# Layer norm of the first segment moved behind the projections: only its mean goes in ahead of the transposes

## The chip, the cores and the metric

The kernel runs on one core of one Trainium2 chip. The metric is the device time of one execution in microseconds (us), as the median of several runs. TensorE (PE) multiplies matrices into PSUM, which has eight banks; VectorE (DVE), ScalarE (ACT) and GpSimd (POOL) do the rest; SyncE (SP) issues the DMAs. Each engine works through its own instructions in order, and waits on semaphores for the others.

## The reference: what is computed

One transformer block on x of 2048 tokens by 1024 features, in two halves. The first half is h = x + A(layernorm(x)), the second h + B(layernorm(h)).

```
# A: 4 segments of 512 tokens, 32 heads of width 32
q, k, v = x @ wq, x @ wk, x @ wv
per segment s:
    p     = softmax(q_s k_s^T * 32**-0.5 + causal mask)
    a_dot = p @ v_s
    a_mem = phi(q_s) M / (phi(q_s) z + 1e-6)      # M, z: sums over the earlier segments
    o_s   = sigmoid(beta) * a_mem + (1 - sigmoid(beta)) * a_dot
    M, z  = M + phi(k_s)^T v_s, z + sum phi(k_s)
A = concat(o_s) @ wo
# B: gelu(x @ w_in), half of it layer-normed and mixed over the tokens by w_sp, times the other half, @ w_out
layernorm(x) = (x - mean(x)) / sqrt(var(x) + 1e-5)  # over the 1024 features of a token
```

The layer norm has no weights of its own. So its factor 1/std belongs to a token: it can be applied to x, or as well to the row of v, and to the column of the transposed q and k, that the token gives.

## The kernel before, in words

The program is written as one list of instructions in source order; a recorder works out the semaphore waits from the tiles that each instruction reads and writes, and puts every instruction at the end of its engine's queue. All instructions have the line of that recorder's call (L209) in the profile, so they are told apart by engine, operation and tiles. A transfer is issued by SP in source order, and waits there for the readers of the tile that it overwrites.

**The opening** works on segment 0, the first 512 tokens, as four chunks of 128 tokens (`XCH[0]` to `XCH[3]`, tile `xch`). SP issues the four loads of x, then the weights: the first half of w_v in two pieces of 256 columns (`WV[0]`), 256 columns each of w_k and w_q, beta, the second half of w_v (`WV[1]`). PE runs 12 idle matmuls on a zeroed tile (`warm(12)`, tile `etmp`), then more of them (`warm(3)`, `warm(2)`) between the first steps. For each chunk:

- `stats_of(tc)`: two BATCH_NORM_STATS2 and one BATCH_NORM_AGGREGATE on DVE (tiles `stats`, `mv`: mean and variance), then two small operations on POOL (tile `rs`: the variance plus epsilon, and that to the power of -0.5).
- `ln_apply`: one DVE operation, x minus the mean times 1/std, to tile `lno`.
- `pe_T`: eight PE transposes of `lno` into PSUM and their copy to the transposed tile `xnT` (by ACT; for the first chunk one half by ACT, the other by DVE).
- `v_quarter`: two groups of eight matmuls (128x256) give half 0 of v for the chunk (columns 0 to 511 of 1024), and ACT copies each group to tile `v`.

For chunk 3 the two `v_quarter` come after `proj_qk(0, 1)` and `proj_qk(0, 0)`, eight matmuls (128x512) each, which give k and q of the first quad transposed; ACT copies them to tile `qk`. `gates()` works out sigmoid(beta) on ACT and DVE. `phi_exp` (ACT) and `phi_max` (DVE, three operations, tiles `pqk` and `etmp`) give phi(k), and SP issues a DMA transpose of it (tile `pk`).

**The quads.** A quad is 4 heads; 8 quads per segment, numbered n = 0 to 31. Quad n is this fixed order of PE work: `logits(n, 0)`; filler f1; `pv(n-1)` (probabilities times v, 40 matmuls); `logits(n, 1)`; `state(n-1)` (phi(k) times v); filler f2; `logits(n, 2)`; filler f3; filler f4. In segment 0 f1 is k and f2 is q of quad n+1, f3 is a 512-column v product. Each `logits` writes PSUM banks 0 to 3, and ACT takes the exponential of all four banks in one instruction (tile `e`), so a `logits` waits for the exponential before it. POOL sets the upper triangle to zero. The fillers take turns with banks 6 and 7. On DVE, quad n has in this order: the norm of quad n-1 after `pv(n-1)` (tiles `rd`, `otok`), two operations after `state` (`msum`, `mzb`), then background work on the next segment's layer norm (`bg_pop`: `stats` of one chunk in each of quads 0 to 3, later its `lno`), then `phi_max(n+1)`. In quad 0 alone, DVE also builds a mask of 13 operations (`mask_g`, tile `maskg`) after the third `logits` and before `phi_max(1)`.

From the second segment on the same quads run with other fillers. Then the second half of the block (tiles `win`, `z`, `z1T`, `wspT`, `w_out`, `yT`), which is PE work end to end, takes the rest of the time.

Of the kernel before, what the change touches and what calls it, by code (L numbers as in the profile page):

```python
# [5 lines left out]
BF16 = mybir.dt.bfloat16  # L6
F32 = mybir.dt.float32
I32 = mybir.dt.int32
ACTF = mybir.ActivationFunctionType
ALU = mybir.AluOpType  # L10

T = 2048
D = 1024
H = 32
NSEG = 4
L = 512
# [3 lines left out]
NQ = 8  # L20
SCALE = 32 ** (-0.5)
LN_EPS = 1e-5
# [235 lines left out]
def bass_sequential_preLN__memory_aug_infini_attn__mixer_gmlp__prompt_kernel(  # L258
# [17 lines left out]
    pe, act, dve, pool, sp = R.pe, R.act, R.dve, R.pool, R.sp  # L276
# [39 lines left out]
    RS = [cb("rs%d" % i, [128, 2], F32) for i in range(4)]  # L316
    RD = cb("rd", [128, 4, 4], F32)
    RDM = cb("rdm", [128, 4, 4], F32)


    HNT = [tens("hnT0", [128, 8, L], BF16, 14 * K), tens("hnT1", [128, 8, L], BF16, 22 * K),
# [8 lines left out]
    HCH = [b1("hch%d" % i, [128, D], BF16) for i in range(3)]  # L330
    LNO = [b1("lno%d" % i, [128, D], BF16) for i in range(3)]
    OT = b1("oT", [128, NQ, L], BF16)
    b2 = Bump(134 * K, ARENA)
    ZSTG = [tens("zstg%d" % i, [128, 448], F32, (134 + 2 * i) * K) for i in range(4)]
    XCH = [b2("xch%d" % i, [128, D], BF16) for i in range(4)]
# [28 lines left out]
    def bank(b):  # L364
        return PS[:, b, :]
# [6 lines left out]
    def next_bank():  # L372
        b = rot["banks"][rot["n"] % len(rot["banks"])]
        rot["n"] += 1
        return b

    def mm8(dst, lhs, rhs, n=8):
        for i in range(n):
            pe.matmul(dst, lhs(i), rhs(i), start=(i == 0), stop=(i == n - 1))
# [5 lines left out]
    def wcols(ap, lo, hi):  # L385
        return ap[:, lo:hi].rearrange("(c p) n -> p c n", p=128)

    for tc in range(4):
        x_load(tc)
    sp.dma_start(WV[0][:, :, 0:256], wcols(A_wv, 0, 256))  # L390
    sp.dma_start(WV[0][:, :, 256:512], wcols(A_wv, 256, 512))
    sp.dma_start(WK[:, :, 0:256], wcols(A_wk, 0, 256))
    sp.dma_start(WQ[:, :, 0:256], wcols(A_wq, 0, 256))
    sp.dma_start(BETAB[:], A_beta.partition_broadcast(128))
# [6 lines left out]
    pool.iota(IOT[:], [[1, 128]], base=0, channel_multiplier=-1)  # L401
    pool.memset(V[:, :, :, 32:34], 1.0)
    pool.memset(BLK[:], 1.0)
    pool.affine_select(out=BLK[:], in_=BLK[:], pattern=[[-32, 4]], compare_op=ALU.is_ge, fill=0.0, base=0,
                       channel_multiplier=1)
    pool.affine_select(out=BLK[:], in_=BLK[:], pattern=[[32, 4]], compare_op=ALU.is_ge, fill=0.0, base=31,
# [20 lines left out]
    def ln_stats(src):  # L427
        k = lnc[0] % 4
        lnc[0] += 1
        for i in range(2):  # L430
            dve.bn_stats(STATS[k][:, i, :], src[:, i * 512:(i + 1) * 512])
        dve.bn_aggr(MV[k][:], STATS[k][:])
        return k

    def ln_rstd(k):
        pool.tensor_single_scalar(RS[k][:, 0:1], MV[k][:, 1:2], float(LN_EPS), ALU.add)
        pool.tensor_tensor(RS[k][:, 1:2], RS[k][:, 0:1], MHALF[:], ALU.pow)
# [3 lines left out]
    def ln_apply(src, k):  # L441
        o = LNO[lno[0] % 3]
        lno[0] += 1
        dve.tensor_scalar(o[:], src[:], MV[k][:, 0:1], RS[k][:, 1:2], ALU.subtract, ALU.mult)
        return o
# [4 lines left out]
    def pe_T(dst, tcl, src, engines=(act,)):  # L450
        w = 8 // len(engines)
        for k, eng in enumerate(engines):
            bb = bank(next_bank()).bitcast(BF16)[:, 0:w * 128]
            for i in range(w):
                o = (k * w + i) * 128
                pe.transpose(bb[:, i * 128:(i + 1) * 128], src[:, o:o + 128], IDENT[:])
            d = dst[:, k * w:(k + 1) * w, tcl * 128:(tcl + 1) * 128]
            v = bb.rearrange("p (c n) -> p c n", c=w)
            if eng is act:
                act.activation(d, v, ACTF.Copy)  # L460
            else:
                dve.tensor_copy(d, v)


    def proj_v(s, tcl, half):
        proj_v_cols(s, tcl, half * 512, 512)

    def proj_v_cols(s, tcl, lo, w):
        b = next_bank()
        xt = XNT[s % 2]  # L470
        mm8(PS[:, b, 0:w], lambda i: xt[:, i, tcl * 128:(tcl + 1) * 128], lambda i: WV[lo // 512][:, i, lo % 512:lo % 512 + w])
        act.activation(V[:, tcl, lo // 32:(lo + w) // 32, 0:32],
                       PS[:, b, 0:w].rearrange("p (h d) -> p h d", d=32), ACTF.Copy)

    def proj_qk(n, which):
        s, c = divmod(n, NQ)
        b = next_bank()
        xt = XNT[s % 2]
        w = WK if which else WQ
        mm8(bank(b), lambda i: w[:, i, c * 128:(c + 1) * 128], lambda i: xt[:, i, :])  # L480
        act.activation(QK[n % 2][:, which, :], bank(b), ACTF.Copy)

    def phi_views(n):
        s = n // NQ
# [17 lines left out]
    def logits(n, rnd):  # L502
        qk = QK[n % 2]
        parts = {0: ((0, 0, 512),), 1: ((1, 0, 384), (3, 384, 128)), 2: ((2, 0, 256),)}[rnd]
        wid = (512, 512, 256)[rnd]
        e = E[n % 2][rnd]
        for j, o, w in parts:
            for i in range(4):
                pe.matmul(PS[:, i, o:o + w], qk[32 * i:32 * (i + 1), 1, j * 128:(j + 1) * 128],
                          qk[32 * i:32 * (i + 1), 0, j * 128:512], start=True, stop=True,  # L510
                          tile_position=(32 * i, 0))
        if rnd == 2 and n >= NQ:
            mem(n)
        act.activation(e[:, :, 0:wid], PS[:, 0:4, 0:wid], ACTF.Exp, scale=float(SCALE))
        for j, o, w in parts:
            d = e[:, :, o:o + 128]
            pool.affine_select(out=d, in_=d, pattern=[[0, 4], [1, 128]], compare_op=ALU.is_ge, fill=0.0,
                               base=0, channel_multiplier=-1)
        if rnd == 2 and n >= NQ:
            mem_norm(n)  # L520
# [84 lines left out]
            lnq[1].append(it + (ln_stats(it[0]),))  # L605


    ks = {}

    def stats_of(tc):  # L610
        ks[tc] = ln_stats(XCH[tc])
        ln_rstd(ks[tc])

    def warm(k):
        for _ in range(k):
            pe.matmul(bank(7), IDENT[:], ETMP[:, 0, :], start=True, stop=True)

    def v_quarter(tcl, q):
        proj_v_cols(0, tcl, 256 * q, 256)

    warm(12)
    stats_of(0)
    stats_of(1)
    ln0 = ln_apply(XCH[0], ks[0])
    pe_T(XNT[0], 0, ln0, (act, dve))
    warm(3)
    ln1 = ln_apply(XCH[1], ks[1])
    stats_of(2)
    pe_T(XNT[0], 1, ln1)
    warm(2)  # L630
    stats_of(3)
    v_quarter(0, 0)
    v_quarter(0, 1)
    ln2 = ln_apply(XCH[2], ks[2])
    ln3 = ln_apply(XCH[3], ks[3])
    pe_T(XNT[0], 2, ln2)
    v_quarter(1, 0)
    v_quarter(1, 1)
    pe_T(XNT[0], 3, ln3)
    v_quarter(2, 0)  # L640
    v_quarter(2, 1)
    for tc in range(4, 8):
        x_load(tc)
    sp.dma_start(WK[:, :, 256:D], wcols(A_wk, 256, D))
    sp.dma_start(WQ[:, :, 256:D], wcols(A_wq, 256, D))
    gates()
    proj_qk(0, 1)
    proj_qk(0, 0)
    v_quarter(3, 0)
    v_quarter(3, 1)  # L650
    phi_exp(0)
    phi_max(0)
    rot["banks"] = [6, 7]
# [39 lines left out]
    for n in range(LAST + 1):  # L693
        s, c = divmod(n, NQ)
        f1, f2, f3, f4 = [], [], [], []
        if n < LAST:
            f1, f2 = [("qk", n + 1, 1)], [("qk", n + 1, 0)]
        if s == 0:
            f3 = [("v", 0, c, 1)] if c < 4 else [("v", 1, c - 4, 0)]
        elif s < NSEG - 1:  # L700
            if c < 2:
                f3, f4 = [("v", s, 2 * c, 1)], [("v", s, 2 * c + 1, 1)]
            elif c < 6:
                f3, f4 = [("wo", s - 1, c - 2, 0)], [("wo", s - 1, c - 2, 1)]
            else:
                f3, f4 = [("v", s + 1, 2 * (c - 6), 0)], [("v", s + 1, 2 * (c - 6) + 1, 0)]
        elif c < 2:
            f3, f4 = [("v", s, 2 * c, 1)], [("v", s, 2 * c + 1, 1)]
        elif c < 6:
            f3, f4 = [("wo", s - 1, c - 2, 0)], [("wo", s - 1, c - 2, 1)]  # L710
        elif c == 6:
            f3, f4 = [("z2", 0, 4, 0)], [("z2", 0, 5, 1)]
        else:
            f1, f2 = [("z2", 0, 6, 2)], [("z2", 0, 7, 3)]
            f3, f4 = [("z2", 0, 0)], [("z2", 0, 1)]

        def fill(lst):
            for u in lst:
                {"v": proj_v, "wo": wo, "qk": proj_qk, "z2": z2_group}[u[0]](*u[1:])

        if s < NSEG - 1 and c < 4:
            ln_tasks(XCH[c], XNT[(s + 1) % 2], c)
        if s < NSEG - 2 and c >= 4:
            x_load(4 * (s + 2) + c - 4)
        if s > 0 and c == 1:
            xr_load(4 * (s - 1))

        logits(n, 0)
        fill(f1)
        if n > 0:  # L730
            pv(n - 1)
        logits(n, 1)
        if n > 0:
            state(n - 1)
        bg_pop()
        fill(f2)
        logits(n, 2)
        if n == 0:
            mask_g()
        if n < LAST:  # L740
            phi_exp(n + 1)
        while n == LAST and staged:
            z2_gelu(*staged.pop(0))
        fill(f3)
        if n < LAST:
            phi_max(n + 1)
        bg_pop()
        fill(f4)
        bg_pop()
        if n == 1:  # L750
            sp.dma_start(WO[:], wcols(A_wo, 0, D))
        if n in (24, 26):
            win_load((n - 24) // 2)
# [101 lines left out]
```

## Time and profile before

| | |
|---|---|
| median of 6 runs | 805.44 us (805.33 to 805.56) |
| the profiled execution's own time | 805.33 us |
| its span in the trace | 803.6 us |
| PE busy | 791.3 us, 98% |
| DVE, ACT, POOL busy | 368.0, 302.9, 121.0 us |
| opening, up to the first `logits` on PE | 0 to 21.89 us |
| quad 0 | 21.89 to 29.16 us |
| quads 1 and 2 | 29.16 to 36.77, 36.77 to 44.37 us |

Busy shares are means over stages. The span is that of the trace; what the measured time has beyond it lies around the span. Times below are microseconds from the span's start. In the timeline a line is a start, a duration, an engine, an operation, its output and inputs and a count; in brackets stands how long the engine had been idle and what released it. A matmul's shown duration holds its way through the array: matmuls of 512 columns start some 0.21 us apart while each is shown with 0.38.

### The profile page before, as it was taken

What the parts mean: (1) busy time and instruction counts of PE and PEld (TensorE: products, weight loads), DVE (VectorE), ACT (ScalarE), POOL (GpSimd) and SP (SyncE); (2) the same over time, 40 slices, a digit from 0 to 9 for tenths busy, and PEclk for the clock granted to TensorE, in tenths of its full rate; (3) what the DMA queues carried; (4) which work ended last, traced back from release to release, by engine and by line L of the source; (5) the groups of instructions that cost most, each with busy time, mean ns of one, the idle gap of its engine ahead of it and who ended that gap; (6) DMA issues with size and microseconds to landing.
All of it is one profiled execution on the core that took longest, in us unless ns stands there. A gap on an engine that the chain in (4) does not pass through costs nothing.

```text
span 803.6 us, 12469 instructions
## 1 busy us (share of the span) xinstructions
PE 791.3 (98%) x5337; PEld 384.1 (48%) x5407; DVE 368.0 (46%) x756; ACT 302.9 (38%) x360; POOL 121.0 (15%) x234
## 2 busy tenths in 40 slices
PE   8999999999999999999999999999999999999998
PEld 5445544555554445455544444444444444444444
DVE  4653688669854675844563000054234323423332
ACT  3888876887787666133333333100000000000000
POOL 2342433234322331100131000000000000000000
PEclk9999999999999999999999999999999999999999
DMA  9672544454415323621116000550270044011002
GB/s 296 157 172 60 92 80 119 80 99 81 99 41 126 113 54 69 188 60 53 53 53 131 1 1 0 194 114 1 79 138 1 26 105 86 1 59 53 1 7 86
DMA packets 125992, 64.79 MB, mean 81 GB/s; under 512 B 94832, under 2 KB 114928, under 8 KB 125936
## 3 DMA queue, kind: packets, MB, share of 16 engines
q1 hardware_dynamic: 125936, 63.99, 33.9%
q8 instruction: 42, 0.69, 0.3%
q14 instruction: 14, 0.11, 0.1%
HBM read 32.51 MB, written 8.39 MB: 51 GB/s over the span
## 4 chain that ended last, share of the span: by engine, by line
PE 92%; DVE 4%; ACT 2%; issue 1%; DMA 0%
PE ps L209 92%; ACT e L209 2%; DVE stats L209 1%; DVE ta L209 0%; DVE otok L209 0%; DVE hch L209 0%; DMA xch<-in_A_x_dram 0%; DVE lno L209 0%; DVE mv L209 0%; DVE rd L209 0%; DVE pqk L209 0%; DVE mzb L209 0%; DVE rdm L209 0%; DVE msum L209 0%; DVE etmp L209 0%
## 5 line engine op out<-in xcount | busy, mean ns | idle before, releaser
L209 PE MATMUL ps<-wspT,z 128*128 128x512 bf16 x878 | 193.1, 379 | 0.9
L209 ACT ACTIVATE e<-ps 128x2048 bf16<-128x2048 f32 (+1 forms) x96 | 152.8, 1591 | 46.1 <-PE ps L209 45.8
L209 PEld LDWEIGHTS ps<-wspT,z 128*128 128x128 bf16 x896 | 87.7, 98 | 105.7
L209 DVE TENSOR_TENSOR tmpg<-ps,brow 128x512 f32<-128x512 f32 x56 | 38.7, 691 | 197.0 <-DMA brow<-in_B_b_sp_dram 104.6
L209 POOL TENSOR_SCALAR_AFFINE_SELECT e<-e 128x512 bf16<-128x512 bf16 x128 | 81.3, 647 | 195.2 <-ACT e L209 195.2
L209 PE MATMUL ps<-win,hnT 128*128 128x448 bf16 x512 | 98.3, 352 | 0.0
L209 PE MATMUL ps<-w_out,yT 128*128 128x512 bf16 (+1 forms) x453 | 96.9, 372 | 0.5
L209 PE MATMUL ps<-hnT,win 128*128 128x512 bf16 x439 | 96.2, 379 | 0.5
L209 PEld LDWEIGHTS ps<-win,hnT 128*128 128x128 bf16 x512 | 49.8, 98 | 46.5 <-issue 0.4
L209 PEld LDWEIGHTS ps<-w_out,yT 128*128 128x128 bf16 x462 | 45.2, 98 | 51.7
L209 PEld LDWEIGHTS ps<-hnT,win 128*128 128x128 bf16 x448 | 43.8, 98 | 52.8
L209 PE MATMUL ps<-xnT,wk 128*128 128x512 bf16 x255 | 60.6, 380 | 0.1
L209 PE MATMUL ps<-wv,xnT 128*128 128x512 bf16 (+1 forms) x288 | 59.0, 356 | 0.0
L209 ACT ACTIVATE z<-ps 128x448 bf16<-128x448 f32 x60 | 32.5, 543 | 69.4 <-PE ps L209 69.4
L209 PE MATMUL ps<-wo,oT 128*128 128x512 bf16 x254 | 57.6, 379 | 0.1
L209 ACT ACTIVATE z1T<-ps 128x512 bf16<-128x512 f32 x56 | 33.4, 597 | 63.3 <-PE ps L209 63.3
L209 PE MATMUL ps<-xnT,wq 128*128 128x512 bf16 x225 | 53.8, 379 | 2.4 <-DVE rd L209 0.6
L209 DVE TENSOR_TENSOR fin<-fin,ps 128x512 bf16<-128x512 bf16 (+1 forms) x33 | 22.1, 672 | 71.5 <-DMA fin<-out_dram 38.7
L209 DVE BATCH_NORM_STATS2 zst<-z 128x6 f32<-128x448 bf16 x64 | 38.9, 620 | 30.1 <-ACT z L209 30.1
L209 ACT ACTIVATE qk<-ps 128x512 bf16<-128x512 f32 x64 | 38.4, 599 | 6.6 <-PE ps L209 6.6
L209 PEld LDWEIGHTS ps<-v,e 128*128 128x128 bf16 x1280 | 36.7, 96 | 7.4
L209 DVE TENSOR_TENSOR yT<-tmpg,z1T 128x512 bf16<-128x512 f32 x56 | 38.8, 692 | 1.9
(67 smaller groups left out, 568.0 us busy)
## 6 DMA issues: line engine op xcount, KB each, us to landing
xch<-in_A_x_dram SPq DMA_DIRECT2D x16, 256.0 KB, 3.6
xr<-in_A_x_dram SPq DMA_DIRECT2D x16, 256.0 KB, 3.7
out_dram<-hch SPq DMA_DIRECT2D x16, 256.0 KB, 2.4
fin<-out_dram SPq DMA_DIRECT2D x16, 256.0 KB, 2.8
out_dram<-fin SPq DMA_DIRECT2D x31, 128.0 KB, 1.7
win<-in_B_w_in_dram SPq DMA_DIRECT2D x4, 896.0 KB, 5.0
w_out<-in_B_w_out_dram SPq DMA_DIRECT2D x1, 3584.0 KB, 12.7
win<-in_B_w_in_dram SPq DMA_DIRECT2D x3, 1024.0 KB, 5.2
```

The costliest lines, as they stand in the source:

```text
L209: ins = getattr(e, op.name)(*op.args, **op.kw)
```

## The change

Segment 0 alone is affected. Its x is centered (the mean is subtracted) before the transposes, and no longer divided by the standard deviation there. 1/std of each token (`RS0`, a column per chunk) is applied later: to v as the scale of the ACT copy out of PSUM (`v_out`), and to k and q, whose tokens lie along the columns, by a DVE multiplication with a tile `RB` that has the 512 values of 1/std in every row (`qk_out`; in the eight quads of segment 0 it takes the place of the ACT copy). `RB` is made by PE: a matrix of ones times two diagonal matrices (`DIAG`, the high and the low part of 1/std in bf16), copied out by ACT.

The means of chunks 1 to 3 come from ACT (`act_mean`: a copy with an accumulator output), and so does the variance of chunk 3 (`act_var`: a square with an accumulator output). Chunks 0 to 2 keep the DVE statistics, chunks 1 and 2 for the variance alone, at a later place. The 128x256 v products become 128x512; those of chunks 0 and 1 go through their eight row blocks side by side, in parts of five and three, with the transposes of chunk 2 between. Half 0 of v for chunk 3 moves into quad 0 as filler f1, and k of quad 1 to the front of `logits(0, 0)`. The first half of w_v is loaded in four pieces of 256 rows. `warm(3)` is gone. For each chunk's transposed halves, the first is copied by ACT and the second by DVE (chunk 0: both by DVE).

```diff
-    sp.dma_start(WV[0][:, :, 0:256], wcols(A_wv, 0, 256))
-    sp.dma_start(WV[0][:, :, 256:512], wcols(A_wv, 256, 512))
+    for i in range(0, 8, 2):
+        sp.dma_start(WV[0][:, i:i + 2, :],
+                     A_wv[i * 128:(i + 2) * 128, 0:512].rearrange("(c p) n -> p c n", p=128))
...
+    pool.memset(ONES[:], 1.0)
...
+    def v_out(s, tcl, half, b):
+        act.activation(V[:, tcl, 16 * half:16 * half + 16, 0:32], bank(b).rearrange("p (h d) -> p h d", d=32),
+                       ACTF.Copy, scale=RS0[tcl][:] if s == 0 else 1.0)
...
-        act.activation(QK[n % 2][:, which, :], bank(b), ACTF.Copy)
+        qk_out(n, which, b)
+
+    def qk_out(n, which, b):
+        if n < NQ:
+            dve.tensor_tensor(QK[n % 2][:, which, :], bank(b), RB[:], ALU.mult)
+        else:
+            act.activation(QK[n % 2][:, which, :], bank(b), ACTF.Copy)
...
+    def center(tc, mean, op=ALU.add):
+        o = LNO[tc % 3]
+        dve.tensor_single_scalar(o[:], XCH[tc][:], mean, op)
+        return o
+    def act_mean(tc):
+        act.activation(JUNK[:], XCH[tc][:], ACTF.Copy, scale=-1.0 / D, accum_out=MEAN[tc][:])
+    def act_var(tc):
+        act.activation(JUNK[:], XCH[tc][:], ACTF.Square, bias=MEAN[tc][:], accum_out=RS[tc][:, 1:2])
+        pool.tensor_scalar(RS[tc][:, 0:1], RS[tc][:, 1:2], 1.0 / D, float(LN_EPS), ALU.mult, ALU.add)
+    def var0(k):
+        pool.tensor_single_scalar(RS[k][:, 0:1], MV[k][:, 1:2], float(LN_EPS), ALU.add)
+    def rstd0(tc):
+        pool.tensor_tensor(RS0[tc][:], RS[tc][:, 0:1], MHALF[:], ALU.pow)
+        pool.tensor_single_scalar(DIAG[0][:, tc, :], IDENT[:], RS0[tc][:], ALU.mult)
+    def diag_lo(tc):
+        dve.scalar_tensor_tensor(DIAG[1][:, tc, :], IDENT[:], RS0[tc][:], DIAG[0][:, tc, :], ALU.mult, ALU.subtract)
...
     warm(12)
-    stats_of(0)
-    stats_of(1)
-    ln0 = ln_apply(XCH[0], ks[0])
-    pe_T(XNT[0], 0, ln0, (act, dve))
-    warm(3)
-    ln1 = ln_apply(XCH[1], ks[1])
-    stats_of(2)
-    pe_T(XNT[0], 1, ln1)
-    warm(2)
-    stats_of(3)
-    v_quarter(0, 0)
-    v_quarter(0, 1)
-    ln2 = ln_apply(XCH[2], ks[2])
-    ln3 = ln_apply(XCH[3], ks[3])
-    pe_T(XNT[0], 2, ln2)
-    v_quarter(1, 0)
-    v_quarter(1, 1)
-    pe_T(XNT[0], 3, ln3)
-    v_quarter(2, 0)
-    v_quarter(2, 1)
+    act_mean(1)
+    var0(ln_stats(XCH[0]))
+    c0 = center(0, MV[0][:, 0:1], ALU.subtract)
+    c1 = center(1, MEAN[1][:])
+    pe_Th(0, c0, dve, dve)
+    act_mean(2)
+    pe_Th(1, c1, act, dve)
+    act_mean(3)
+    rstd0(0)
+    c2 = center(2, MEAN[2][:])
+    var0(ln_stats(XCH[1]))
+    rstd0(1)
+    act_var(3)
+    c3 = center(3, MEAN[3][:])
+    warm(2)
+    vb = [next_bank() for _ in range(2)]
+    for i in range(5):
+        for t in range(2):
+            v_mm(0, t, 0, vb[t], i)
+    pe_Th(2, c2, act, dve)
+    rstd0(3)
+    var0(ln_stats(XCH[2]))
+    rstd0(2)
+    diag_lo(0)
+    for i in range(5, 8):
+        for t in range(2):
+            v_mm(0, t, 0, vb[t], i)
+    pe_Th(3, c3, act, dve)
+    v_out(0, 0, 0, vb[0])
+    diag_lo(1)
+    diag_lo(3)
+    diag_lo(2)
+    v_out(0, 1, 0, vb[1])
+    proj_v(0, 2, 0)
+    bk, bq, br = next_bank(), next_bank(), next_bank()
+    mm8(bank(bk), lambda i: WK[:, i, 0:128], lambda i: XNT[0][:, i, :])
+    for i in range(2):
+        pe.matmul(bank(br), ONES[:], DIAG[i][:].rearrange("p c n -> p (c n)"), start=(i == 0), stop=(i == 1))
+    act.activation(RB[:], bank(br), ACTF.Copy)
+    qk_out(0, 1, bk)
+    mm8(bank(bq), lambda i: WQ[:, i, 0:128], lambda i: XNT[0][:, i, :])
+    qk_out(0, 0, bq)
...
     gates()
-    proj_qk(0, 1)
-    proj_qk(0, 0)
-    v_quarter(3, 0)
-    v_quarter(3, 1)
     phi_exp(0)
     phi_max(0)
...
+        if n == 0:
+            fill(f1)
+            f1 = [("v", 0, 3, 0)]
         logits(n, 0)
         fill(f1)
```

## Prediction of the time after

> **What bounds the kernel now.** I read the page first, for the engine that is full.
>
> ```profile
> PE 791.3 (98%) x5337; PEld 384.1 (48%) x5407; DVE 368.0 (46%) x756; ACT 302.9 (38%) x360; POOL 121.0 (15%) x234
> PEclk9999999999999999999999999999999999999999
> ```
>
> PE fills the span at the full granted clock; the idle time can only lie in the opening. Then the chain of waits in order of time (start, length, what), for where PE waited and until when.
>
> ```profile
> 0.79 2.62 DMA xch<-in_A_x_dram
> ...
> 5.10 0.57 DVE stats L209
> ...
> 6.63 0.42 DVE lno L209
> 7.05 0.05 issue
> 7.09 0.63 PE ps L209 x8
> ...
> 11.73 0.42 DVE lno L209
> 12.15 0.05 issue
> 12.20 4.56 PE ps L209 x48
> ...
> 22.90 1.77 ACT e L209
> 24.67 0.49 ACT qk L209
> 25.16 0.02 issue
> 25.17 1.89 ACT e L209
> 27.06 0.05 issue
> 27.11 5.95 PE ps L209 x76
> 33.05 0.05 issue
> 33.11 7.55 PE ps L209 x83
> 40.66 0.05 issue
> 40.71 7.55 PE ps L209 x83
> ```
>
> Up to 12.20 VectorE's statistics set the end, from 22.90 to 27.06 ScalarE's exponentials in quad 0, and from 27.11 PE runs without a gap: quad after quad 7.60 us (40.71 less 33.11). So a time saved before that point is saved whole, if nothing in the quads starts to wait. Last VectorE's timeline in quad 0, since the change gives it work there:
>
> ```profile
> 25.18 0.75 DVE L209 COPY maskg<-gs 128x1024 f32<-128x1024 f32 x1
> 25.97 1.93 DVE L209 TENSOR_SCALAR maskg<-maskg,blk 128x256 f32<-128x256 f32 x4
> 27.93 1.51 DVE L209 COPY maskg<-blk 128x4 f32<-128x4 f32 x8
> ...
> 30.26 0.55 DVE L209 TENSOR_SCALAR lno<-xch,mv,rs 128x1024 bf16<-128x1024 bf16 x1
> 32.42 0.26 DVE L209 RECIPROCAL rd<-ps 128x16 f32<-128x16 f32 x1 [1.61 <-PE ps L209]
> ```
>
> The mask, phi of quad 1 and `lno` are one block of 5.6 us (25.18 to 30.81); then VectorE waits 1.61 us for PE. This is all the cover that work added behind the mask has.
>
> **The opening, part by part.** *Chunk 0.* Its statistics end at 5.10 as now; centering follows at once (0.42, the step of `lno` in the chain), so `lno` is there at 5.55, not 7.05. The two POOL operations leave the path. But PE is in its 12 idle matmuls: the last starts at 6.26, and they start 0.43 apart, so PE is free at 6.69. What is late next is therefore the idle block, and the first transposes gain 0.40, not 1.5.
>
> *Chunk 1* needs ScalarE's mean. x of chunk 1 lands at 4.05 (issue 1.25 plus 2.8). A ScalarE pass over 1024 elements with an accumulator is not in the trace: from below 1.02 (`xnT`, 1024 elements), from above 1.87 (2048 elements). I take 1.1, nearest to the first: done by 5.2, centered by 6.0, before PE is free. So PE does 16 transposes from 6.69 to 7.55 (0.43 per eight, as 7.09 to 7.50) and `warm(2)` to 7.98. Copies out: the first half is ready 0.44 after the first transpose, the second 0.66 (7.53 and 7.75 against 7.09). VectorE takes chunk 0's at 7.13 and 7.5 (0.42 each), ends 7.9; ScalarE chunk 1's first half 7.57 to 8.17, VectorE the second to 8.3. So v starts at 8.0, with a hitch to 8.2. Of w_v, 0.5 MB landed at 8.25 and 10.03 before; in row pieces of 0.25 MB behind x (6.48) they come 0.7 to 0.9 us apart, about 7.3, 8.1, 8.9, 9.8, each before the matmul that needs it (8.0, 8.8, 9.7, 11.0). Two more issues on SP (0.45 each) push w_k and w_q into a ring that is full anyway (their issues take 2.56 and 1.59); they landed at 11.86 and 13.46 and are now needed at 14.0 and 16.1. The loads of chunks 4 to 7 wait for the last reader of `xch`: chunk 2's is now its statistics, done 12.8 (it was `lno`, near 12.2); then the same transfers follow as now.
>
> *Chunks 2 and 3.* On ScalarE: means at 6.9 and 9.2, the square to 10.4. On VectorE, in order: centering of chunk 2 (8.3 to 8.7), statistics of 1 (1.6, to 10.3), centering of 3 (10.7), half of chunk 2's copies (11.2), statistics of 2 (12.8), `diag_lo` (0.25: between 0.17, `ident`, and 0.43, `pqk`), half of chunk 3's copies (13.45), three `diag_lo`, the last held by POOL to 14.4 (add 0.25, power 0.6, diagonal 0.3, between 0.24 for `iot` and 0.64 for `e`). PE: ten matmuls of 0.215 from 8.0 and the hitch to 10.1, eight transposes (chunk 2 centered for 1.4 us already), six matmuls to 11.83, eight transposes to 12.27, v of chunk 2 to 13.99, k to 15.7, two ones-matmuls to 16.14 (0.43, new), q to 17.86, k of quad 1 to 19.58. All cover holds: ScalarE 1.1 us at chunk 3's centering, VectorE's second half for k's fifth matmul 1.4 us, the diagonals 1.3 us. `RB` is out at 16.95 (0.60), k multiplied by 17.7, q by 18.76 (0.69: every VectorE operation on 128x512 PSUM with a second operand, `tmpg` 691 ns, `otok` 0.69). So **quad 0's first logits start at 19.58**, against 21.89 with k of quad 1 still to come: 4.0 us ahead in work done; the missing v product of chunk 3 (1.7) comes back at once, into time in which PE waited for ScalarE (0.60 in the trace).
>
> If both ScalarE sums take the upper end, chunk 1's copy is 0.25 late and chunk 2's, queued behind the square, 0.25 again: 0.5 in all. If the diagonals take 0.65 the last ends at 15.1, still covered.
>
> The page "ScalarE: Activation LUTs" of the Trainium skill, section "Table sets: the hidden batching unit", lists the functions that every set holds without the square, and "What ACT_TABLE_LOAD costs" puts a switch at 2.66 us; the trace has one load, 1.28 us, at the start. By that rule the square would end near 13.0, chunk 2's copy 13.6, v of chunk 2 would start 1.3 us late, and the gain below would shrink by that; the second load, before beta's exponential, falls into free time. I stay with no load.
>
> **Quad 0 and the backlog.** From the first logits at L = 19.58: ScalarE starts the exponential 0.40 later (21.89 to 22.28 on PE), takes 1.87, PE goes on 0.05 later: 21.9. The v product fills 1.7 of these 2.3 us. Second logits 0.33, q of quad 1 1.72: its matmuls end at 23.96, its multiplication runs 24.17 to 24.86. The mask follows it. From the mask's start to the end of `lno` the trace has 5.54 (overlap taken off), so the multiplication of quad 2's k, queued behind, runs 30.4 to 31.05. It must free PSUM bank 6 for q of quad 2, **which starts at 31.1**; PE alone would be there at 30.2. So VectorE takes back 0.9 of 2.7. Before, that q started at 32.89 (four `state` matmuls from 32.64). Gain 1.8.
>
> **After that.** In quad 1 VectorE has the norm (1.64 from reciprocal to statistics), statistics (1.55) and quad 2's q (0.69): to 34.9, when PE has just ended its v product (34.8); logits of quad 2 at 34.95 against 36.76, again 1.8. From quad 2 on: statistics end 6.55 us after a quad's first logits (43.32 less 36.77), the q multiplication 7.25, next logits 7.60: 0.35 to spare in quads 1 to 3, 1.9 later, when the statistics are gone. ScalarE is relieved of 1.2 us per quad; it was not the bound there, so nothing is gained.
>
> Sum: 805.33 less 1.79 is 803.54 for an execution like the profiled one (its span 803.60, 1.73 around it); the median lies 0.11 higher: **803.65**. What a measurement can tell from no change is 0.2%, 1.61 us; the line is 803.83, inside my forecast's own range of 803.2 to 804.1.
>
> **Rivals.**
> - *The backlog does not bind* (the mask's block shortens, or its work fits earlier): PE reaches q at 30.2, gain 2.7, 802.75. Against it: VectorE's order is fixed, and the mask cannot start before that multiplication. 0.10.
> - *The opening slips* and most of the gain goes: sums on ScalarE at the upper end (0.5 late), or a table load, or idle matmuls no longer bridging PE's pauses; gain 0.3 to 1.5, 803.9 to 805.1. For: three engines now hand over within 0.1 to 1.4 us. 0.22.
> - *It does not do what it says*: PE is held until 7.05 or later anyway and the ones-matmuls and the backlog eat the rest; 805.4. 0.06.
> - *Slower: the column multiplications on VectorE.* If one takes 1.38, twice the 691 ns, two of them lengthen the block before q of quad 2 (1.4 lost), and the q multiplication in quads 1 to 3 ends 0.5 to 1.0 after PE wants it, some 2.0 in all: 1.6 slower, 807.1. It decides from about 1.05 each. Against: the trace's two-operand rows with PSUM (`tmpg`, `hch`, `fin`, `tm`, `ta`, `otok`) have means of 680 to 692 ns. 0.10.
>
> The trace has the idle matmuls 0.43 apart to 6.26 and 0.22 at 7.5. "TensorE: Matmul & The Clock Gate" of the Trainium skill ("What's actually happening") says that activity of about 3.4 us lifts PE from half clock and that the moment varies: if it came after 6.69, 16 transposes would cost up to 0.9 more, gain 0.9. It speaks against taking `warm(3)` out; no row here shows it.
>
> **Numbers.** Forecast 0.52, of which 0.42 lies under 803.83. Faster 0.42 + 0.10 = 0.52; the same 0.10 + 0.22 + 0.06 = 0.38; slower 0.10. The range takes all but the slower case and the tails: 802.7 to 805.4.
>
> **What would show it.** First transposes at 6.7; 16 without a pause; v from 8.2 with no gap to the first logits at 19.6; `maskg` right behind a `qk` multiplication near 24.9; PE idle 0.9 us before q of quad 2, released by VectorE's `qk`; 7.60 us a quad after. Wrong if the multiplication is not near 0.69, a second table load appears before 16, or PE waits in quads 2 and 3.

## The result, and the profile after

The changed kernel takes 803.24 us, the median of 19 runs (802.76 to 805.04); the kernel before takes 805.36 in the runs beside them (39 runs). The ratio is 0.9976, with a 95% interval of 0.9970 to 0.9982: faster by 2.1 us where 1.8 were forecast (803.65). The profiled execution took 803.43, with a span of 801.7 against 803.6.

The engines' shares hardly move. From the page of the changed kernel:

```profile
PE 790.0 (99%) x5304; PEld 380.9 (48%) x5374; DVE 380.3 (47%) x777; ACT 298.2 (37%) x348; POOL 124.8 (16%) x239
```

VectorE works 12.3 us more (380.3 less 368.0), 11.0 of it the 16 multiplications of q and k at 0.69, and the kernel is faster all the same. The chain of waits of the changed kernel, in order of time (start, length, what):

```profile
2.65 5.39 DMA wv<-in_A_wv_dram
...
8.18 3.04 PE ps L209 x19
...
11.27 9.17 PE ps L209 x50
...
20.46 1.89 ACT e L209
...
24.66 0.69 DVE qk L209
25.35 0.64 DVE maskg L209
...
29.60 0.80 DVE lno L209
30.40 0.60 DVE qk L209
30.99 0.18 DVE rd L209
...
31.28 7.55 PE ps L209 x83
...
38.88 7.55 PE ps L209 x83
```

The statistics are gone from the head of the chain. In their place stand the load of w_v (to 8.04) and, behind the first exponential, VectorE's block: q of quad 1, the mask, phi of quad 1, `lno`, k of quad 2. PE's timeline of the changed kernel gives the dates:

```profile
6.13 1.06 PE L209 MATMUL ps<-ident,lno 128*128 128x128 bf16 x16
...
8.18 2.38 PE L209 MATMUL ps<-wv,xnT 128*128 128x512 bf16 x10 [0.56 <-DMA wv<-in_A_wv_dram]
...
20.02 0.39 PE L209 MATMUL ps<-qk 32*128 32x512 bf16 x4
...
31.28 1.67 PE L209 MATMUL ps<-xnT,wq 128*128 128x512 bf16 x7 [0.54 <-DVE rd L209]
...
34.94 0.39 PE L209 MATMUL ps<-qk 32*128 32x512 bf16 x4
```

PE waits 0.56 us for w_v, has no gap from 8.18 to the first logits at 20.02, and waits 0.54 us before q of quad 2 (seven of its eight matmuls are in the trace; the first weights are loaded at 31.05, when k's multiplication, done at 30.99 in the chain, has freed the bank; the `rd` named as releaser only follows it). Logits of quad 2 start at 34.94 against 36.77 before, 1.83 earlier, and those of quad 3 at 42.54: 7.60 us a quad, as before.

### The profile page after: what moved, and what is told of

It is laid out like the page before. It is cut to its first block, busy times and chain, and to the rows that moved or that the text cites. A ratio compares the mean times of both kernels' runs of the same rounds, so it can differ in the third digit from the quotient of the medians.

```text
span 801.7 us, 12431 instructions
## 1 busy us (share of the span) xinstructions
PE 790.0 (99%) x5304; PEld 380.9 (48%) x5374; DVE 380.3 (47%) x777; ACT 298.2 (37%) x348; POOL 124.8 (16%) x239
## 4 chain that ended last, share of the span: by engine, by line
PE 92%; DVE 4%; ACT 2%; issue 1%; DMA 1%; SPq 0%
PE ps L209 92%; ACT e L209 2%; DMA wv<-in_A_wv_dram 1%; DVE stats L209 1%; DVE maskg L209 0%; DVE ta L209 0%; DVE otok L209 0%; DVE hch L209 0%; DVE pqk L209 0%; DVE rd L209 0%; DVE lno L209 0%; SPq L209 0%; DVE qk L209 0%; DVE mzb L209 0%; DVE etmp L209 0%
## 5 line engine op out<-in xcount | busy, mean ns | idle before, releaser
L209 PE MATMUL ps<-wv,xnT 128*128 128x512 bf16 x254 | 58.7, 379 | 0.8 <-DMA wv<-in_A_wv_dram 0.6
L209 PEld LDWEIGHTS ps<-wo,oT 128*128 128x128 bf16 x256 | 24.5, 98 | 27.2
```

Of the source, the lines that this page charges most:

```text
L209: ins = getattr(e, op.name)(*op.args, **op.kw)
```

## The experiments

**Theory A** is the chain above: a start set by w_v and by the copies of chunk 1, PE without a gap from there, and a block on VectorE that takes back half a microsecond. Its rivals: B, the gain comes from the statistics path (the power out of chunk 0's way, 1.6 us of VectorE per chunk); C, it comes from the new fillers of quad 0. All kernels start from the changed one unless another is named. With the same opening the v products began at 7.43 to 8.37 us in the traces of different kernels, as w_v landed and as PE's idle matmuls came to follow each other faster; so differences of 0.3 us between medians are not read as effects.

### The mask before the multiplication

```diff
         bg_pop()
+        if n == 0:
+            mask_g()      # its broadcast copy and four multiplications
         fill(f2)
         logits(n, 2)
         if n == 0:
-            mask_g()
+            mask_b()      # its eight small copies
```

> The mask is split: its broadcast copy and four multiplications run on VectorE before q of quad 1 is multiplied (VectorE waits 1.85 us there in the changed kernel), only the eight small copies stay behind. Theory A (VectorE's block behind the mask holds q of quad 2, by the 0.5 us that PE is idle there): that wait goes, 0.4 to 0.6 us faster than the changed kernel, about 802.7. Theory B (the block is not what PE waits for; ScalarE's exponentials or the DMA transpose of phi(k) end about then and take its place): no change, 803.2. If the mask's first part runs over the end of q of quad 1, the logits of quad 1 wait instead and 0.2 of the gain goes.

Measured: 802.80 us (802.30 to 803.43), ratio 0.9969 (0.9957 to 0.9981). The chain of waits of this kernel:

```profile
22.58 1.78 ACT e L209
...
24.41 5.95 PE ps L209 x76
...
30.40 7.55 PE ps L209 x83
```

After the second exponential PE runs from 24.41 through q of quad 2 (30.40) with no wait, and VectorE is no longer in the chain. The medians differ by 0.44 us, which is what theory A priced but little more than the openings' scatter. The trace is the stronger evidence: from the first logits (19.63) to q of quad 2 it takes 10.77 us where the changed kernel takes 11.26, so the wait of 0.5 us was the block's.

### w_v in columns again

```diff
-    for i in range(0, 8, 2):
-        sp.dma_start(WV[0][:, i:i + 2, :], ...)      # 256 rows
+    sp.dma_start(WV[0][:, :, 0:256], wcols(A_wv, 0, 256))
+    sp.dma_start(WV[0][:, :, 256:512], wcols(A_wv, 256, 512))
```

> The first half of w_v is loaded again in two pieces of 256 columns, all else as changed. The v products of 512 columns then need both pieces for their first matmul. Theory A (from the v products on PE runs without a pause, and their start is set by w_v's first piece, 8.04 us): the start moves to the second piece's landing, 10.03 us in the kernel before, and all after it by the same: 1.9 us slower than the changed kernel, about 805.1. Theory B (the statistics set the start, w_v has slack): 0 to 0.5 slower.

Measured: 805.98 us (805.29 to 807.40), slower than the kernel before (ratio 1.001, 1.0002 to 1.0019). From PE's timeline of this kernel:

```profile
10.50 2.32 PE L209 MATMUL ps<-wv,xnT 128*128 128x512 bf16 x10 [1.87 <-DVE stats L209]
```

The second piece lands at 10.3 (the `stats` named as releaser only end at about that time), the v products start at 10.50 against 8.18, 2.3 later, and so does all that follows (span 804.0 against 801.7). Theory A: once the products are 512 columns wide, the row pieces carry the whole gain. The medians differ by 2.7. Seven of the eleven executions list a mean granted clock of 1.0, and their median is 805.71, 2.5 above the changed kernel. The other four list 0.998 and took 807.03 to 807.40; they lift the median by the rest.

### Chunk 0 normed in full

```diff
-    var0(ln_stats(XCH[0]))
-    c0 = center(0, MV[0][:, 0:1], ALU.subtract)
+    ln_rstd(ln_stats(XCH[0]))
+    dve.tensor_scalar(c0[:], XCH[0][:], MV[0][:, 0:1], RS[0][:, 1:2], ALU.subtract, ALU.mult)
...
-    rstd0(0)
+    pool.memset(RS0[0][:], 1.0)
+    pool.tensor_single_scalar(DIAG[0][:, 0, :], IDENT[:], RS0[0][:], ALU.mult)
```

> Chunk 0 is normed in full before its transposes, as in the kernel before (POOL's two operations on the path, 1.3 us), and its later factor is set to one; all else as changed. Theory A (w_v's first piece sets the start of the v products, chunk 0 has over 1 us to spare): PE's first transposes come at about 6.9 in place of 6.13, the v products 0 to 0.4 us later: 803.2 to 803.6. Theory B (the prediction's first term: taking chunk 0's power off the path is what brings the opening forward): the whole 0.8 us is lost, 804.0.

Measured: 803.37 us (803.22 to 803.55), 0.13 above the changed kernel, which is within the openings' scatter. From the chain of this kernel:

```profile
6.16 0.56 DVE lno L209
...
6.76 4.38 PE ps L209 x37
```

The first transposes come at 6.76 in place of 6.13, and PE goes on without a pause to the v products at 8.16, where the changed kernel's start at 8.18, behind w_v. So theory B fails for chunk 0, but two floors lie side by side: 0.13 is the price of chunk 0's path next to this load. In an execution in which w_v lands earlier, it could cost more.

### Sums back on VectorE

```diff
-    act_mean(1)
     var0(ln_stats(XCH[0]))
     c0 = center(0, MV[0][:, 0:1], ALU.subtract)
-    c1 = center(1, MEAN[1][:])
+    var0(ln_stats(XCH[1]))
+    c1 = center(1, MV[1][:, 0:1], ALU.subtract)
...  # chunks 2 and 3 likewise, their statistics just ahead of their centering
```

> The sums go back from ScalarE to VectorE: all four chunks have their statistics there, in the order statistics, centering, and ScalarE only copies. Theory A (the start of the v products has a floor of its own, at w_v's landing and the copies of chunk 1): chunk 1 is centered at 7.5 in place of 6.0, its copies end at 8.6 in place of 8.4, chunks 2 and 3 are centered near 10.6 and 12.6, just where PE wants them: 0.2 to 0.6 slower than the changed kernel, 803.4 to 803.8. Theory B (each statistic of 1.6 us taken off VectorE is a gain): 1.5 or more slower, 804.8.

Measured: 804.50 us (804.41 to 804.57), 1.26 slower: nearer to B's number than to mine. PE's timeline of this kernel shows why:

```profile
7.92 0.62 PE L209 MATMUL ps<-ident,lno 128*128 128x128 bf16 x8 [1.46 <-DVE lno L209]
...
8.81 2.32 PE L209 MATMUL ps<-wv,xnT 128*128 128x512 bf16 x10
...
13.25 0.62 PE L209 MATMUL ps<-ident,lno 128*128 128x128 bf16 x8 [0.18 <-DVE lno L209]
```

Chunk 1 is centered at 7.87 (I had 7.5), the v products start at 8.81, 0.63 late; then chunk 2 and chunk 3 are centered at 11.1 and 13.2, each just after PE wants them (0.2 us of wait each time). So it is no 1.6 us per chunk, but the sum of three small delays: without ScalarE's sums VectorE is the bound of the opening at every step.

### The v product of chunk 3 before quad 0

```diff
+    proj_v(0, 3, 0)
     gates()
     phi_exp(0)
...
-        if n == 0:
-            fill(f1)
-            f1 = [("v", 0, 3, 0)]
```

> The v product of chunk 3 goes back to the end of the opening, and k of quad 1 is again the filler behind the first logits; all else as changed. Theory A: only two products of 1.72 us have changed places, the first logits start when they did and have a filler as long: 0 to 0.2 slower than the changed kernel, 803.2 to 803.4. Theory C (the filler in ScalarE's exponential is where the time comes from, the 0.60 us that PE waited there before): 0.5 to 0.7 slower, 803.8 to 803.9.

Measured: 804.29 us (803.73 to 804.67), 1.05 slower. My expectation fails, and C's price is too small. ScalarE's timeline of this kernel:

```profile
20.25 0.69 ACT L209 ACTIVATE v<-ps,rs 128x512 bf16<-128x512 f32 x1 [2.86 <-PE ps L209]
20.84 0.22 ACT L209 ACTIVATE gs<-betab 128x32 f32<-128x32 bf16 x1
20.96 0.62 ACT L209 ACTIVATE etmp<-qk 128x512 bf16<-128x512 bf16 x1
21.48 1.87 ACT L209 ACTIVATE e<-ps 128x2048 bf16<-128x2048 f32 x1
```

ScalarE waits 2.86 us for the v product; beta's and phi's exponentials are queued behind its copy though their inputs are long there, and the first exponential starts 1.33 us after its logits (20.15) in place of 0.44. PE waits 1.02 for it. That gave a new theory: the order of ScalarE's queue, not the filler. Two kernels test it.

The same, with ScalarE's copy behind the first exponential:

```diff
-    proj_v(0, 3, 0)
+    for i in range(8):
+        v_mm(0, 3, 0, v3_bank, i)      # matmuls alone
...
         logits(n, 0)
+        if n == 0:
+            v_out(0, 3, 0, v3_bank)
```

> As with the v product of chunk 3 put back before quad 0, but ScalarE's copy of it is queued behind the first exponential. New theory (the 1.02 us that PE waited there came from ScalarE's queue: the v copy, which waits for the product, stood ahead of beta's exponential, of phi's and so of the first exponential, which began 1.3 us after its logits in place of 0.44): the wait goes, 803.2 to 803.6. Rival (PE needs the v product itself as filler at that place, whatever ScalarE's order): it stays at 804.3.

Measured: 803.68 us (803.01 to 804.13); span 801.5. The first exponential starts 0.45 after its logits again (19.83 after 19.38), and the 1.02 are gone. This trace had an early opening (v products at 7.61). From the first logits to those of quad 2 it takes 15.39 us where the changed kernel takes 14.92: 0.26 more because q of quad 1 waits for the bank that this copy frees, and 0.21 in VectorE's block. So ScalarE's order accounts for the wait of 1.02. The 0.44 that is left between the medians is not only the openings' scatter; how much of it the edit causes is open, since the 0.21 lie in one operation (0.91 in place of 0.43) beside a POOL triangle operation.

And that part of the change alone, in the kernel before:

```diff
-    v_quarter(3, 0)
-    v_quarter(3, 1)
...
+        if n == 0:
+            fill(f1)
+            f1 = []
         logits(n, 0)
+        if n == 0:
+            v_quarter(3, 0)
+            v_quarter(3, 1)
```

> The kernel before, with one part of the change alone: the v product of chunk 3 becomes the filler of quad 0, and k of quad 1 comes in front of its first logits. By the new theory it depends on ScalarE's queue: there k of quad 1 is still copied by ScalarE (0.60), ahead of the first exponential, which starts at about 22.5 in place of 22.8: 0.2 to 0.5 faster than the kernel before, 804.9 to 805.2. If the place of the filler is what counts, about 1.0 faster, 804.4.

Measured: 805.04 us (804.79 to 805.15), 0.34 below the kernel before beside it (805.38); the interval of the ratio, 0.9986 to 1.0004, includes no change, though all its eleven executions (up to 805.15) lie below all twenty beside them (from 805.21). k of quad 1 is copied by ScalarE at 22.14, and the first exponential waits for it to 22.64. So the new order is worth some 0.3 us in the kernel before, as expected, and 1.05 in the changed one. That the difference comes from the multiplications on VectorE, which take ScalarE's copies of q and k out of its queue, is read from this timeline and was not tested by itself.

### The multiplication twice over

```diff
-            dve.tensor_tensor(QK[n % 2][:, which, :], bank(b), RB[:], ALU.mult)
+            for _ in range(2):
+                dve.tensor_tensor(QK[n % 2][:, which, :], bank(b), RB[:], ALU.mult)
```

> Every column multiplication of q and k in segment 0 is done twice over, with the same result, so that each costs about 1.3 us on VectorE. By the prediction's slower rival, priced from the changed kernel's trace: the block before q of quad 2 is longer by two of them (1.3 us), then q in quads 1 to 3 ends 0.5 us late each time, since these have the statistics ahead of it, and nothing in quads 4 to 7: 2.5 to 3.0 us slower than the changed kernel, 805.7 to 806.2, slower than the kernel before. If instead VectorE has room in the quads, as its idle time of 2.7 us in a quad would have it, only the first 1.3 is lost: 804.5.

Measured: 807.11 us (806.66 to 807.77), ratio 1.0021 (1.0012 to 1.003): more than I had expected. From the stages view of this kernel (2 us each: us, busy time of PE, its weight loads, VectorE, ScalarE, POOL, then the granted clock, the DMA engines' share and GB/s), and from the timelines of PE and VectorE:

```profile
30.00:32.00 2.00, 0.14 (x2) 0.21 (x3) 1.93 (x5) 1.61 (x1) 0.33 (x1) 1.00 0.32 66
32.00:34.00 2.00, 2.00 (x6) 0.71 (x5) 1.93 (x5) 0.00 (x0) 0.90 (x2) 0.54 0.69 131
34.00:36.00 2.00, 2.00 (x10) 0.54 (x9) 1.90 (x5) 0.83 (x1) 0.00 (x0) 0.60 0.00 0
36.00:38.00 2.00, 2.00 (x13) 0.75 (x12) 1.67 (x4) 1.48 (x4) 1.66 (x3) 1.00 0.03 8
```

```profile
31.88 2.90 PE L209 MATMUL ps<-xnT,wq 128*128 128x512 bf16 x7 [1.86 <-DVE rd L209]
...
35.09 1.36 DVE L209 TENSOR_TENSOR qk<-ps,rb 128x512 bf16<-128x512 f32 x2
...
37.12 0.40 PE L209 MATMUL ps<-qk 32*128 32x512 bf16 x4
...
45.35 0.39 PE L209 MATMUL ps<-qk 32*128 32x512 bf16 x4 [0.53 <-DVE qk L209]
```

The block makes PE wait 1.86 us before q of quad 2, and after that pause the granted clock is 0.54 and 0.60 in the two stretches from 32 to 36. From that q (first weights at 31.65) to the next quad's logits (37.12) PE needs 5.47 us where it needed 3.89. Not all of these 1.58 are the clock's. VectorE, busy without a pause since 24.12, ends the second multiplication of quad 2's q at 36.45, and the logits could not have started before; PE at its usual pace would have been there at 35.54 (31.65 plus 3.89). So 1.0 is VectorE's in any case, and 0.6 is the clock's.

Against the changed kernel: the block 1.3 (two more multiplications), VectorE in quad 1 1.0, the clock 0.6, quads 2 and 3 at 8.2 us each 1.2 more; 4.1, less a start that was 0.7 earlier, is the 3.4 by which the spans differ (805.1, 801.7). In quads 4 to 7 nothing is lost. The low clock is not what makes the median: the profiled execution and three others list a mean of 0.998 and have a median of 806.94, the other seven list 1.0 and have 807.20. How early those started is not known, since they have no trace.

### Further versions

w_v's first piece ahead of chunk 3 of x, on top of the early mask:

```diff
-    for tc in range(4):
+    for tc in range(3):
         x_load(tc)
     for i in range(0, 8, 2):
+        if i == 2:
+            x_load(3)
         sp.dma_start(WV[0][:, i:i + 2, :], ...)
```

> The split mask, and w_v's first row piece issued ahead of chunk 3 of x. Theory A (the landing of that piece sets the start of the v products in some executions, 8.04 us in the changed kernel's): it lands 0.5 to 0.8 earlier, and the start is set by the copies of chunk 1 and the idle matmuls: 0.1 to 0.4 faster than with the split mask alone, 802.4 to 802.7. If the landing does not count: 802.8. If chunk 3 of x, now later by as much, holds its own centering: slower than 802.8.

Measured: 802.59 us (802.47 to 802.97), ratio 0.9965 (0.9952 to 0.9979), the fastest run here, but not to be told from the early mask alone (802.30 to 803.43). In its trace the first piece lands at 6.8, and the v products start at 8.24, right behind the idle matmuls, which had ended late (first transposes at 6.69).

Then with ScalarE's copy ahead of chunk 2's mean:

```diff
-    act_mean(2)
     pe_Th(1, c1, act, dve)
+    act_mean(2)
     act_mean(3)
```

> As the one before, and ScalarE copies chunk 1's transposes ahead of chunk 2's mean, which waits for x (6.75 to 7.90 in the changed kernel, with the copy held behind it to 8.38). Theory A: the copy is done by 7.6, the v products start at 7.2 to 7.6 without the hitch: 0.2 to 0.5 faster than without, 802.0 to 802.4. Against it: mean, square and chunk 2's copy move back by 0.6, and the last diagonal may come after PE wants it (15.2 to 15.5 against 16.0 in the changed kernel): then no faster.

Measured: 803.24 us (802.81 to 804.21): no faster, the median 0.65 above the run before it. In the trace the v products do start at 7.57, and then wait 0.58 us for w_v's second piece, which lands at 9.12; later PE waits once more, for the DMA transpose of phi(k), to 30.55. There the earlier start only meets the transfers.

## Why the prediction was right, and where not

- **What bounds, and what carries to the end**: held. 1.83 us at quad 2's logits, 7.60 us a quad after, 1.9 in the span.
- **"The first transposes gain 0.40"**: 6.13 in place of 6.69, since PE's idle matmuls followed each other faster from about 5.4 on (their weights were loaded 0.43 apart to 5.13, then closer). In the traces that date varies, 5.73 to 6.84. More to the point, this gain hardly carries on: with chunk 0 normed in full the transposes start at 6.76, and the median is 0.13 us higher. The step that the prediction credited here gains little beside w_v's load.
- **"So v starts at 8.0, with a hitch to 8.2"**: 8.18, but by the load; the copy of chunk 1 that I had named for the hitch ended right behind it, at 8.38. I put w_v's first row piece at 7.3; it landed at 8.04, and chunks 2 and 3 of x at 6.7 and 7.4 in place of 5.7 and 6.5. In the other traces with the same transfers in the same order the piece landed between 7.35 and 8.25, so this floor moves from one execution to the next, and the cover that I gave w_v from one trace is there in some and not in others.
- **First logits at 19.58**: 20.02, 0.44 late, from that start and small hand-overs. No wait between: ScalarE's sums took 1.06 plus 0.19 for reading the accumulator (I had 1.1), `diag_lo` 0.35, POOL's diagonal 0.62 (near my upper end), the last diagonal done at 15.5, before PE wants it at 16.03. There is no second table load in the opening; the square took 1.15. The Trainium skill's list of functions in every table set ("ScalarE: Activation LUTs", "Table sets: the hidden batching unit") does not name the square; here it ran under the exponential's table without a switch.
- **"VectorE takes back 0.9 of 2.7"**: it took back 0.5 of 2.3. The block from the mask to the end of `lno` is 5.13 us, not 5.54: the eight small copies took 0.67 in place of 1.51, `lno` 0.88 in place of 0.55. q of quad 2 was forecast at 31.1 and its first weights load at 31.05: the late opening and the short block cancelled. The early mask shows that the wait was the block's.
- **"0.35 to spare in quads 1 to 3"**: held (7.60 us a quad; in quad 2 q's multiplication ends at 42.05, 0.49 before the next logits). With twice the multiplication quads 2 and 3 lose 0.6 each: the second one of k pushes the norm back by 0.35, the second one of q takes 0.7, and the spare covers the rest.
- **The slower rival** was given 807.1 at 1.38 us per multiplication, and that kernel takes 807.11. Its terms come out too: the block is the 1.3 to 1.4 foreseen, and VectorE's lateness in quads 1 to 3 is 1.0 and twice 0.6, 2.2 where 2.0 were foreseen. The clock was not in the sum; in the profiled execution its 0.6 and a start 0.7 earlier cancel, which is luck.
- **Left out**: that ScalarE's queue in quad 0 was part of the gain. I counted the moved v product as filler (it is), not that its copy would otherwise stand ahead of the first exponential: 1.05 us. With the sums on ScalarE (1.26) and the row pieces (2.5), three parts are each worth about half of the whole gain or more, and none of them is the factor moved off chunk 0's path. They don't add up: each is what the others need. Norming chunks 1 to 3 in full with the rest as changed was not tried, nor were the side-by-side order of the first v products and the sharing of the transposes' copies taken back by themselves.

## What to carry to other kernels

Before crediting a shorter path, look for the next floor under it, transfers first: here the power off chunk 0's path was worth 0.13 us, the way w_v is cut 2.5. When work changes engine, read both queues in order: a copy that waits for a late product holds up every ready instruction behind it, and a block on the engine that receives the work can stand where a bank is to be freed. Take back the small part that is movable (the mask, a wait of 0.5 us) before looking for more. And before charging a low clock with lost time, look for the engine that would have held the path anyway: of 1.58 us here, 1.0 was VectorE's.

## What the runs showed of the hardware

- After a pause of PE of 1.86 us (twice the multiplication) the granted clock was 0.54 and 0.60 in two stretches of 2 us, and PE took 1.58 us longer to the next logits; 0.6 of it lay on the path. "TensorE: Matmul & The Clock Gate" of the Trainium skill ("What's actually happening") has the clock fall after an idle window of about 3.4 us; the pause here is about half of that, with only small matmuls (`state`) just ahead of it. Pauses of 0.54 left the clock at 1.00, and so did one of 1.87 in the profiled execution with w_v in columns, while four other executions of that kernel list a mean of 0.998 and took 1.6 us more than the rest: whether it falls is not settled by length alone.
- `lno`, 0.55 us otherwise, took 0.88 where a POOL triangle operation had started 0.04 us ahead of it (29.48 against 29.52), and in the kernel before one of the small mask copies took 0.64 in place of 0.16 where such an operation ran from 28.57. That POOL holds VectorE up is read from these overlaps, and was not tested by itself.
- Reading out a ScalarE accumulator is an instruction of its own, 0.19 us behind each sum.
- The 2 MB of x and the first half of w_v were in at about 9.6 to 10.6 us in the nine traces with four row pieces, and at 10.0 to 10.3 in the three with two column pieces: the cut decides which part comes first more than when all is there.
